# One block of a transformer on one NeuronCore: the second token tile of four pairs turned on VectorE instead of TensorE, with features dealt 5p+b

## The chip, the cores and the metric

The kernel runs on one core of one Trainium2 chip. The metric is the device time of one execution in microseconds (us); smaller is better. Three runs of the kernel before gave 762.3, 762.86 and 761.41 us, with a median of 762.3 us. The engines are named as the profile names them: PE is TensorE's matmul, PEld its weight load, DVE is VectorE, ACT is ScalarE, POOL is GpSimd, and SP is the engine whose queue issues most transfers.

## The reference

The kernel computes one block with two halves, conditioned by a vector c, for S = 2048 tokens of D = 640 features. All arrays are fp32.

```python
mod = silu(c) @ w_mod                      # six vectors of 640: sa, ca, ga, sb, cb, gb
h = layernorm(x) * (1 + ca) + sa
q, k, v = h @ wqkv                         # 32 heads of 20
phi_q = concat(softmax(q @ w_phi), softmax(-q @ w_phi))     # by head; phi_k alike
o = phi_q @ (phi_k.T @ v) / (phi_q @ sum(phi_k))
x = x + ga * (o @ wo)
h = layernorm(x) * (1 + cb) + sb
x = x + gb * (relu(h @ w1 + b1)**2 @ w2 + b2)
```

## The kernel before

**Tiles.** Tokens stand in 16 tiles of 128, and two tiles make a pair j (0 to 7). Matmuls contract over the partitions, so LayerNorm's result, which has tokens on the partitions, has to be turned first: 640 features are five chunks d = 0 to 4 of 128. Every fp32 factor is split into a high part and a rest (`hi`, written by ACT, and `lo`, the difference, written by DVE), and a product is three matmuls: hi by hi, hi by lo, lo by hi. That is `three`, and `proj` strings 15 of them (5 chunks by 3) for the first 384 output columns and 15 for the other 256.

**Phase 1** is the loop over tiles t = 2 to 13 (j, i = t // 2, t % 2), behind a start written by hand for pairs 0 and 1. For each tile PE does k, v and q, each with `proj`. In the tile with i = 0 it also adds the products of keys and values of the two tiles before (`do_kv`, output `kvp`). In between PE turns the next pair: chunks 0 and 1 behind q of the first tile (`t1(j + 1, 0, 1)`), chunks 2 and 3 between v and q of the second, and chunk 4 inside q of the second, 12 matmuls before its end. The next thing on PE is k of the next pair's first tile, which reads all five chunks in order.

`t1` is `t_in` (one transpose on PE for each tile and chunk, into the PSUM tile `ta`) and `t_out`: ACT writes `hf` = scaled and shifted `ta` (128x256, both tiles at once), ACT copies `hf` into `hT` (the high part), DVE subtracts (`lo`, the rest).

**LayerNorm** of a pair is `ln_parts`: sums on ACT, a factor on POOL, squares on ACT, three small operations on POOL, and a scaling of both tiles on ACT. It ran in the pair's predecessor, in the tile with i = 0.

**DVE** in phase 1 has, for each tile: maxima and minima by head of k and q (`mxk`, `mxq`), differences (`ek`, `eq`), sums of the exponentials (`sk`, `rs_q`), the reciprocal, the normalization of `ek` by `sk`, and `lo` of `hT`. It also sums w_mod by rows (`wm`) and prepares wo (`rwo`).

**What sets the order.** PE's order in the loop is the program's (`manual_schedule` for PE alone). DVE, ACT, POOL and SP are ordered by the scheduler, which simulates a timeline; each engine then runs its list strictly in that order.

**Where features stand.** Before, chunk d of phase 1 is features 128d to 128d+127. The second half of the kernel already uses the other order, chunk b holding features 5p+b (`by_turn`), and from its pair 1 on has its turns done by DVE in 32x32 blocks (`turn`, `ln_dealt`, `load_dealt`).

Of the kernel before, what the change touches and what calls it, by code (L numbers as in the profile page):

```python
# [21 lines left out]
NT = S // P  # L22
NC = D // P
# [9 lines left out]
EPS = 1e-5  # L33
# [19 lines left out]
def kernel(  # L53
# [54 lines left out]
    def tok2(tag, name, at=0, pool=None):  # L108

        bufs = 1  # L110
        if tag == "w":
            tag = f"w{next(w_at)}"
        elif pool is None:
            bufs = BUFS.get(tag, 1)
        t = (pool or mem).tile([P, 2 * D + (W2_AT if tag == 'late' else 128 if tag in W_LONG else 0)], F32, tag=tag, name=name, bufs=bufs)
        return t[:, at : at + 2 * D].rearrange("p (s d) -> p s d", s=2)

    def row(tag, name):
        return (pc if tag in ("s3", "s4") else mem).tile([P, D], F32, tag=tag, name=name, bufs=BUFS[tag])
# [7 lines left out]
    def ht(name, j, at=(32, 0)):  # L127

        t = mem.tile([P, NC * 512 + (32, 96)[j % 2]], F32R, tag=f"h{j % 2}", name=name, bufs=1)
        at = at[j % 2]  # L130
        return t[:, at : at + NC * 512].rearrange("p (d s n) -> p d s n", d=NC, s=2)

    def small(shape, tag, name, bufs=2):
        return (pc if tag in ("mx", "sk", "dn", "dd") else tiny).tile(shape, F32, tag=tag, name=name, bufs=bufs)
# [4 lines left out]
    def tp(name):  # L139
        return psA.tile([P, 512], F32, tag="tp", name=name)  # L140
# [80 lines left out]
    def load_x(j):  # L221
        XB[j] = tok2(f"x{j % 2}", f"xb{j}")
        nc.sync.dma_start(XB[j], x[256 * j : 256 * j + 256].rearrange("(i p) d -> p i d", p=P))

    def load_wm(d):
        WM[d] = flat(tok2(("k", "k", "q0", "q1", "w")[d], f"wm_{d}"))
# [106 lines left out]
    def ln_parts(xt, nm, spare=None):  # L333
        sm = small([P, 2], "sm", f"sm{nm}")
        sq = small([P, 2], "sq", f"sq{nm}")
        nb = small([P, 2], "nb", f"nb{nm}")
        for i in range(2):
            same = spare[i] if spare else xt[:, i] if nm[0] == "a" else row("s3", f"same{nm}_{i}")
            nc.scalar.activation(same, xt[:, i], AF.Identity, accum_out=sm[:, i : i + 1])
        nc.gpsimd.tensor_scalar(sm, sm, -1.0 / D, None, op0=ALU.mult)  # L340
        yield
        for i in range(2):
            junk = spare[i] if spare else row("s3", f"junk{nm}_{i}")
            nc.scalar.activation(junk, xt[:, i], AF.Square, bias=sm[:, i : i + 1], accum_out=sq[:, i : i + 1])
        nc.gpsimd.tensor_scalar(sq, sq, 1.0 / D, EPS, op0=ALU.mult, op1=ALU.add)
        nc.gpsimd.tensor_tensor(sq, sq, mhalf, op=ALU.pow)
        nc.gpsimd.tensor_tensor(nb, sm, sq, op=ALU.mult)
        yield
        for i in range(2):
            nc.scalar.activation(xt[:, i], xt[:, i], AF.Identity, bias=nb[:, i : i + 1], scale=sq[:, i : i + 1])  # L350
        yield

    def layer_norm(xt, nm, spare=None):
        for _ in ln_parts(xt, nm, spare):
            pass

    def by_turn(ap):
        return ap.rearrange("p (f b) -> p b f", b=NC)

    def t_in(xn, d, p, mixed=False):  # L360
        for i in range(2):
            src = by_turn(xn[:, i])[:, d] if mixed else xn[:, i, d * P : (d + 1) * P]
            nc.tensor.transpose(p[:, i * P : (i + 1) * P], src, ident)  # L363

    def t_unit(xn, cols, hT, d, nm, p=None):
        if p is None:
            p = tp(f"t{nm}_{d}")
        t_in(xn, d, p, True)
        t_out(cols, hT, d, nm, p)

    def t_out(cols, hT, d, nm, p, hf=None):
        if hf is None:
            hf = row("s3", f"hf{nm}_{d}")[:, :256]
        nc.scalar.activation(hf, p[:, :256], AF.Identity, bias=cols[:, d : d + 1], scale=cols[:, 5 + d : 6 + d])
        nc.scalar.activation(hT[:, d, 0], hf, AF.Copy)
        lo(hT[:, d, 1], hf, hT[:, d, 0])

# [5 lines left out]
    def newest(engine):  # L383
        return next(i for i in reversed(nc.cur_bb.bb.instructions) if i.engine == engine)

    DONE = []

    def t1(j, *ds, more=None):
        if 0 in ds:
            HT[j] = ht(f"hT{j}", j)  # L390
        p = tp(f"ta{j}_{ds[0]}")
        for k, d in enumerate(ds):
            t_in(XB[j], d, p[:, 256 * k : 256 * k + 256])
        if more:
            mod_turn(more[0], p[:, 256:], 4)
        for k, d in enumerate(ds):
            t_out(cols_a, HT[j], d, f"a{j}", p[:, 256 * k : 256 * k + 256])
        DONE[:] = newest(ET_.Activation), newest(ET_.DVE)
        if more:
            mod_sum(*more)  # L400

    def proj(nm, t, between=None):
        p = pj(f"p{nm}{t}")
        j, i = divmod(t, 2)
        s = slice(i * P, (i + 1) * P)
        for h, (a, b) in enumerate(CUT):
            terms = []
            for d in range(NC):
                w = W[nm, d]
# [308 lines left out]
    for t in range(2, NT - 2):  # L718
        j, i = divmod(t, 2)
        if i == 0 and j < NT // 2 - 2:  # L720
            load_x(j + 2)
        PK[t] = row("s2", f"k{t}")
        to_sb(proj("k", t), PK[t])
        if t == NT - 4:
            t1(j + 1, 0, 1)
        norm = j + 1 if i == 0 and t < NT - 4 else j + 2 if t == NT - 5 else None
        if norm:
            if not i:
                parts = ln_parts(XB[norm], f"a{norm}")
            with tc.issue_after(newest(ET_.Activation)):  # L730
                next(parts)
        p = proj("v", t, (1, 0, lambda: t1(j + 1, 4)) if t == NT - 3 else None)
        if i == 0:
            do_kv(t - 2)
            do_kv(t - 1)
            if t in AFTER_KV:
                AFTER_KV[t]()
        v_out(t, p)
        if norm and not i:
            next(parts)  # L740
        EK[t] = tok2("k", f"ek{t}")
        spread(PK[t], EK[t], f"k{t}")
        exps(EK[t])
        if norm and not i:
            next(parts)
        if i and t < NT - 4:
            t1(j + 1, 2, 3)
        with tc.issue_after(newest(ET_.DVE)):
            k_norm(EK[t], t)
        if t < NT - POSTPONED:  # L750
            do_q(t, (1, 3, lambda: t1(j + 1, 4, more=LAST_COL.get(t))) if i else None)
            if norm and i:
                with tc.issue_after(newest(ET_.Activation)), tc.issue_after(DONE[0]):
# [12 lines left out]
        SIDE[t]()  # L766
# [305 lines left out]
    def t2(j, *ds):  # L1072
        if 0 in ds:
            H2[j] = ht(f"h2_{j}", j, (0, 96))
        if j == 0:
            t_unit(XM[j], cols_b, H2[j], ds[0], f"b{j}", bank(f"tb{j}_{ds[0]}"))
            return
        if j in DEALT:
            for d in ds:
                hf = XM[j].rearrange("p s d -> p (s d)")[:, 256 * d : 256 * d + 256]  # L1080
                t_out(cols_b, H2[j], d, f"b{j}", hf, hf)
            return
        p = tp(f"tb{j}_{ds[0]}")
        for k, d in enumerate(ds):
            t_in(XM[j], d, p[:, 256 * k : 256 * k + 256], True)
        for k, d in enumerate(ds):
            t_out(cols_b, H2[j], d, f"b{j}", p[:, 256 * k : 256 * k + 256], XX[j][d % 2][:, :256])

# [663 lines left out]
```

## Time and profile before

| | us |
|---|---|
| median of three runs | 762.3 |
| lowest, highest | 761.41, 762.86 |
| the profiled execution, device time | 760.53 |
| its span, first to last instruction | 758.8 |
| phase 1's loop, in the span | about 60 to 226 |
| PE busy there | 166.00 of 166.00 |
| DVE busy there | 148.09 of 166.00 |
| ACT busy there | 113.92 of 166.00 |

All durations used below come from the one profiled execution, and its time is 1.8 us under the median of the runs. A row of the timeline gives start, length, engine, line, operation, output and input, shape and count; in square brackets stands how long the engine was idle before and who released it. Consecutive instructions of one engine overlap a little, so steps are taken from start to start.

### The profile page before, as it was taken

To read this page: it belongs to the slowest core of one execution; us is meant where nothing else is said; L and a number is where in the kernel's file an instruction comes from. 1 tells how busy PE (TensorE), PEld (TensorE's weight loads), DVE (VectorE), ACT (ScalarE), POOL (GpSimd) and SP (SyncE) were. 2 spreads that over 40 slices of the span, in tenths; PEclk is the share of its full clock that TensorE was granted. 3 is DMA by queue.
4 is the path that set the end of the run, shared out by engine and by line. 5 is a ranking of instruction groups with operands and counts; after the bars stand their busy time and mean duration, and the time that the engine had idled before them with its cause. 6 is when DMAs were issued, how large, how long until landed. Compare 5 with 4: busy or idle time off the path is not lost.

```text
span 758.8 us, 15386 instructions
## 1 busy us (share of the span) xinstructions
PE 751.5 (99%) x5898; PEld 732.2 (96%) x5898; DVE 605.3 (80%) x1121; ACT 456.7 (60%) x1054; POOL 168.7 (22%) x349
## 2 busy tenths in 40 slices
PE   9999999999999999999999999999999999999997
PEld 9999999999999988998999999999999999999997
DVE  6598997988999899998655868777777776777766
ACT  5767666677853365555777656466474756647431
POOL 3001101011100247543413020132221313213110
PEclk9999999999999999999999999999999999999999
DMA  9812431342332354644886555997677777767461
GB/s 328 329 57 83 139 105 54 105 137 103 137 105 94 94 167 149 164 105 105 208 206 213 141 191 212 283 273 214 186 206 209 205 196 201 207 177 216 125 182 36
DMA packets 57778, 126.04 MB, mean 166 GB/s; under 512 B 7324, under 2 KB 15265, under 8 KB 57705
## 3 DMA queue, kind: packets, MB, share of 16 engines
q1 hardware_dynamic: 37554, 78.75, 31.5%
q0 software_dynamic: 17568, 41.00, 21.9%
q10 hardware_dynamic: 2583, 5.30, 1.8%
q8 instruction: 46, 0.75, 0.4%
q14 instruction: 27, 0.22, 0.1%
HBM read 100.29 MB, written 29.89 MB: 172 GB/s over the span
## 4 chain that ended last, share of the span: by engine, by line
PE 87%; DVE 9%; ACT 3%; issue 1%; POOL 0%; DVEq 0%; POOLq 0%
PE up L79 22%; PE acc L79 16%; PE pq L79 9%; PE pk L79 9%; PE pv L79 9%; PE pwo L79 6%; PE acc3x L79 4%; PE kvp L455 3%; PE te L925 1%; DVE dn L883 1%; DVE scr L881 1%; DVE ezb L905 1%; PE ta L363 1%; DVE ot L89 1%; PE foldq L281 1%
## 5 line engine op out<-in xcount | busy, mean ns | idle before, releaser
L79 PE MATMUL up<-h,w 128*128 128x256 f32 x1640 | 204.6, 277 | 1.2 <-ACT ft L1268 0.9
L79 PEld LDWEIGHTS up<-h,w 128*128 128x128 f32 x1640 | 196.3, 188 | 2.1 <-ACT ft L1268 1.2
L1268 ACT ACTIVATE ft<-up,b_t 128x256 f32<-128x256 f32 x104 | 48.8, 470 | 97.4 <-PE up L79 97.2
L79 PE MATMUL acc<-w,ra 128*128 128x384 f32 x452 | 97.9, 336 | 0.6 <-DVE ra L89 0.6
L79 PE MATMUL pwo<-wo,ot 128*128 128x256 f32 (+3 forms) x512 | 80.6, 312 | 0.1
L1269 DVE TENSOR_TENSOR ft<-ft 128x256 f32<-128x256 f32 x104 | 43.9, 422 | 44.2 <-ACT ft L1268 42.8
L79 PEld LDWEIGHTS pwo<-wo,ot 128*128 128x128 f32 (+1 forms) x512 | 74.4, 188 | 3.2 <-issue 2.7
L79 PE MATMUL pq<-wq,hT 128*128 128x384 f32 (+1 forms) x480 | 75.1, 312 | 0.0
L79 PEld LDWEIGHTS acc<-w,ra 128*128 128x128 f32 x452 | 72.8, 188 | 1.9 <-DVE ra L89 1.7
L79 PE MATMUL pk<-wk,hT 128*128 128x384 f32 (+1 forms) x480 | 72.7, 309 | 0.0
L79 PE MATMUL pv<-wv,hT 128*128 128x384 f32 (+1 forms) x480 | 71.6, 307 | 0.0
L79 PEld LDWEIGHTS pq<-wq,hT 128*128 128x128 f32 x480 | 71.0, 188 | 0.6 <-issue 0.2
L79 PEld LDWEIGHTS pk<-wk,hT 128*128 128x128 f32 x480 | 70.5, 188 | 0.4 <-issue 0.2
L79 PEld LDWEIGHTS pv<-wv,hT 128*128 128x128 f32 x480 | 70.0, 188 | 0.0
L89 DVE TENSOR_TENSOR ra<-ft,ra 128x384 fp32r<-128x384 f32 (+2 forms) x86 | 36.8, 449 | 32.5 <-ACT ra L1292 19.9
L1378 POOL DMA_DIRECT2D ring_a<-td_a x34 | 18.5, 544 | 116.7 <-PE acc L79 105.6
L1292 ACT ACTIVATE ra<-ft 128x384 fp32r<-128x384 f32 x48 | 25.2, 526 | 28.4 <-DVE ft L1269 22.3
L79 PE MATMUL acc3x<-w,ra 128*128 128x256 f32 x231 | 39.8, 279 | 0.0
L79 PEld LDWEIGHTS acc3x<-w,ra 128*128 128x128 f32 x231 | 37.3, 188 | 0.2 <-DVE ra L89 0.2
L1283 DVE TENSOR_TENSOR ft<-ft 128x128 f32<-128x128 f32 x136 | 33.4, 287 | 1.2
L446 DVE TENSOR_REDUCE sk<-ek 128x64 f32<-128x1280 f32 x16 | 23.7, 1484 | 12.4 <-ACT ek L441 10.8
L889 POOL TENSOR_TENSOR dn<-dn,rs_q 128x32 f32<-128x32 f32 x32 | 20.1, 629 | 60.1 <-DVE dn L883 59.8
(274 smaller groups left out, 1454.1 us busy)
## 6 DMA issues: line engine op xcount, KB each, us to landing
ring_c<-td_c POOLq DMA_DIRECT2D x34, 384.0 KB, 3.9
ring_a<-td_a POOLq DMA_DIRECT2D x34, 384.0 KB, 3.4
ring_b<-td_b POOLq DMA_DIRECT2D x34, 256.0 KB, 3.4
esp<-eq SPq DMA_DIRECT2D x12, 640.0 KB, 3.1
el<-esp SPq DMA_DIRECT2D x12, 640.0 KB, 4.3
rw<-in_w SPq DMA_DIRECT2D x23, 320.0 KB, 3.5
wm<-in_w_mod SPq DMA_DIRECT2D x20, 320.0 KB, 3.4
xb<-in_x SPq DMA_DIRECT2D x8, 640.0 KB, 4.1
```

The source lines that it names most:

```text
L79: nc.tensor.matmul(o, a, b, start=first and i == 0, stop=last and i == len(terms) - 1, skip_group_check=skip,)
L89: (eng or nc.vector).tensor_tensor(out_lo, full, hi.bitcast(F32), op=ALU.subtract)
L281: nc.tensor.matmul(p[g // 3][:, (g % 3) * 120 : (g % 3) * 120 + n], r, bd_t[:120, g * 120 : g * 120 + n], start=True, stop=True,)
L363: nc.tensor.transpose(p[:, i * P : (i + 1) * P], src, ident)
L446: nc.vector.tensor_reduce(s, heads(flat(e)), axis=AX.X, op=ALU.add)
L455: nc.tensor.matmul(kvp[g // 4][64 * c : 64 * c + 64, a : a + 2 * n].rearrange("p (s n) -> p s n", s=2), v[:, u], e[:, :, o : o + n], start ...
L889: nc.gpsimd.tensor_tensor(dn[:, s], dn[:, s], rs[:, 1 - s], op=ALU.mult)
L1268: nc.scalar.activation(r, p, AF.Relu, bias=b1_t[:, f : f + 1])
L1269: nc.vector.tensor_tensor(r, r, r, op=ALU.mult)
L1283: nc.vector.tensor_tensor(t[:, o], t[:, a], t[:, b], op=op)
L1292: nc.scalar.activation(a[:, 0, :3], t[:, :3], AF.Copy)
L1378: nc.gpsimd.dma_start(RING[j, n, r], TD[n][r].bitcast(F32R))
```

## The change

Pairs 3 to 6 (`EARLY_DEALT`) no longer have their second tile turned by PE. Its x is loaded a second time, dealt over the partitions by four transfers: 32 tokens to a group of partitions, four runs of 160 features. `dealt_parts` replaces `ln_parts` for these pairs. It starts one tile earlier, in the second tile of pair j-2. POOL copies each token's two factors to where the dealt rows need them (16 copies of 32x4), ACT scales the dealt tile in four pieces of 160 columns, and one DVE transpose of 32x32 blocks writes the turned tile over the second half of `xb`. So that a block transpose yields whole chunks, all of phase 1 now has chunk b hold features 5p+b, and the weights and modulation rows are put in that order on the host. PE's remaining transposes read every fifth column. `t_out` has two inputs for these pairs, `ta` for the first tile and `xb` for the second, so its one 128x256 ACT operation becomes two of 128x128.

```diff
+EARLY_DEALT = range(3, NT // 2 - 1)
     def load_x(j):
         XB[j] = tok2(f"x{j % 2}", f"xb{j}")
         nc.sync.dma_start(XB[j], x[256 * j : 256 * j + 256].rearrange("(i p) d -> p i d", p=P))
+        if j in EARLY_DEALT:
+            XD[j] = row("s4", f"xd{j}")
+            for q in range(4):
+                nc.sync.dma_start(
+                    XD[j][32 * q : 32 * q + 32].rearrange("t (a c) -> t a c", a=4),
+                    x[256 * j + P : 256 * j + 2 * P, 160 * q : 160 * q + 160].rearrange("(a t) c -> t a c", a=4),
+                )
+    def dealt_parts(j):
+        xt, junk = XB[j], row("s3", f"junka{j}")
+        sm = small([P, 2], "sm", f"sma{j}")
+        rn = tiny.tile([P, 2, 2], F32, tag="rn", name=f"rna{j}", bufs=1)
+        ra = tiny.tile([P, 4, 2, 2], F32, tag="rna", name=f"rnaa{j}", bufs=1)
+        sq, nb = rn[:, :, 0], rn[:, :, 1]
+        for i in range(2):
+            nc.scalar.activation(junk, xt[:, i], AF.Identity, accum_out=sm[:, i : i + 1])
+        nc.gpsimd.tensor_scalar(sm, sm, -1.0 / D, None, op0=ALU.mult)
+        yield
+        for i in range(2):
+            nc.scalar.activation(junk, xt[:, i], AF.Square, bias=sm[:, i : i + 1], accum_out=rn[:, i, 0:1])
+        nc.gpsimd.tensor_scalar(sq, sq, 1.0 / D, EPS, op0=ALU.mult, op1=ALU.add)
+        nc.gpsimd.tensor_tensor(sq, sq, mhalf, op=ALU.pow)
+        nc.gpsimd.tensor_tensor(nb, sm, sq, op=ALU.mult)
+        for a in range(4):
+            for q in range(4):
+                nc.gpsimd.tensor_copy(ra[32 * q : 32 * q + 32, a], rn[32 * a : 32 * a + 32])
+        yield
+        for a in range(4):
+            d = XD[j][:, 160 * a : 160 * a + 160]
+            nc.scalar.activation(d, d, AF.Identity, bias=ra[:, a, 1, 1:2], scale=ra[:, a, 1, 0:1])
+        yield
+        nc.scalar.activation(xt[:, 0], xt[:, 0], AF.Identity, bias=rn[:, 0, 1:2], scale=rn[:, 0, 0:1])
+        yield
+        with tc.issue_after(newest(ET_.DVE)):
+            nc.vector.transpose(xt[:, 1].rearrange("p (b a t) -> p a b t", b=NC, t=32), XD[j].rearrange("p (a t b) -> p a b t", a=4, t=32))
+        yield
-    def t_in(xn, d, p, mixed=False):
-        for i in range(2):
-            src = by_turn(xn[:, i])[:, d] if mixed else xn[:, i, d * P : (d + 1) * P]
-            nc.tensor.transpose(p[:, i * P : (i + 1) * P], src, ident)
+    def t_in(xn, d, p):
+        for i in range(xn.shape[1]):
+            nc.tensor.transpose(p[:, i * P : (i + 1) * P], by_turn(xn[:, i])[:, d], ident)
...
-        nc.scalar.activation(hf, p[:, :256], AF.Identity, bias=cols[:, d : d + 1], scale=cols[:, 5 + d : 6 + d])
+        for o, p in ((hf, p[:, :256]),) if second is None else ((hf[:, :P], p[:, :P]), (hf[:, P:], second)):
+            nc.scalar.activation(o, p, AF.Identity, bias=cols[:, d : d + 1], scale=cols[:, 5 + d : 6 + d])
...
+        deal = i and j + 2 in EARLY_DEALT
+        if deal:
+            DEAL[j + 2] = dealt_parts(j + 2)
+            with tc.issue_after(newest(ET_.Activation)):
+                next(DEAL[j + 2])
```

**What moves on ACT and DVE.** The scheduler orders both anew. The three places below lie where PE goes from q of a pair's second tile to k of the next pair. First, ACT at t = 7 (pair 3's second tile), from the turn of chunks 2 and 3 to that of chunk 4, before (`hfa_2` to `hfa_4` are `hf` of the chunks, `ek` the exponentials of k, `mt` a modulation column):

```order
L374 ACTIVATE hfa_2_1777<-ta_2_1772,cols_a 128x256
L374 ACTIVATE hfa_3_1781<-ta_2_1772,cols_a 128x256
L441 ACTIVATE ek_1764<-ek_1764 128x640
L375 ACTIVATE hT_1673<-hfa_2_1777 128x256
L375 ACTIVATE hT_1673<-hfa_3_1781 128x256
L442 ACTIVATE ek_1764<-ek_1764 128x640
L431 ACTIVATE q_1831<-pq_0_1789 128x384
L308 ACTIVATE mt_1597<-ta_4_1809 128x128
L374 ACTIVATE hfa_4_1814<-ta_4_1809,cols_a 128x256
L375 ACTIVATE hT_1673<-hfa_4_1814 128x256
```

and now, from the second piece of chunk 3 on (ahead of it stand the two pieces `hfa_2<-ta_2` and `hfa_3<-ta_2`, with one `ek` between them):

```order
L411 ACTIVATE hfa_3_1861<-xb_1188,cols_a 128x128
L372 ACTIVATE junka_1781,rna_1783<-xb_1556,sma_1782 128x640
L412 ACTIVATE hT_1726<-hfa_2_1856 128x256
L412 ACTIVATE hT_1726<-hfa_3_1861 128x256
L469 ACTIVATE q_1912<-pq_0_1870 128x384
L479 ACTIVATE ek_1845<-ek_1845 128x640
L316 ACTIVATE mt_1657<-ta_4_1890 128x128
L411 ACTIVATE hfa_4_1894<-ta_4_1890,cols_a 128x128
L411 ACTIVATE hfa_4_1894<-xb_1188,cols_a 128x128
L469 ACTIVATE q_1912<-pq_1_1871 128x256
L384 ACTIVATE xb_1556<-xb_1556,rna_1783 128x640
L412 ACTIVATE hT_1726<-hfa_4_1894 128x256
```

The high part of chunk 4 (the last row) now has a square, the eviction of q's last columns and the scaling of the pair after next's first tile ahead of it, and the second `ek` stands behind q's first columns.

DVE at the same place, before:

```order
L438 TENSOR_TENSOR ek_1764<-k_1693,mxk_1765 128x640
L89 TENSOR_TENSOR hT_1673<-hfa_2_1777,hT_1673 128x256
L89 TENSOR_TENSOR hT_1673<-hfa_3_1781,hT_1673 128x256
L446 TENSOR_REDUCE sk_1785<-ek_1764 128x64
L89 TENSOR_TENSOR hT_1673<-hfa_4_1814,hT_1673 128x256
L312 TENSOR_REDUCE gate_a<-mt_1597 128x5
L447 RECIPROCAL sk_1785<-sk_1785 128x64
```

and now:

```order
L476 TENSOR_TENSOR ek_1845<-k_1746,mxk_1846 128x640
L90 TENSOR_TENSOR hT_1726<-hfa_2_1856,hT_1726 128x256
L90 TENSOR_TENSOR hT_1726<-hfa_3_1861,hT_1726 128x256
L484 TENSOR_REDUCE sk_1866<-ek_1845 128x64
L485 RECIPROCAL sk_1866<-sk_1866 128x64
L486 TENSOR_TENSOR ek_1845<-ek_1845,sk_1866 128x1280
L90 TENSOR_TENSOR hT_1726<-hfa_4_1894,hT_1726 128x256
```

The rest of chunk 4 moved behind the reciprocal and the normalization of `ek`. At t = 3, 5, 9 and 11 it still stands directly behind the sum `sk`.

Third, ACT at t = 5 (pair 2's second tile), before:

```order
L375 ACTIVATE hT_1322<-hfa_2_1426 128x256
L375 ACTIVATE hT_1322<-hfa_3_1430 128x256
L441 ACTIVATE ek_1413<-ek_1413 128x640
L442 ACTIVATE ek_1413<-ek_1413 128x640
L431 ACTIVATE q_1477<-pq_0_1438 128x384
L374 ACTIVATE hfa_4_1461<-ta_4_1458,cols_a 128x256
L375 ACTIVATE hT_1322<-hfa_4_1461 128x256
```

and now:

```order
L372 ACTIVATE junka_1406,rna_1408<-xb_1188,sma_1407 128x640
L479 ACTIVATE ek_1470<-ek_1470 128x640
L412 ACTIVATE hT_1351<-hfa_2_1481 128x256
L412 ACTIVATE hT_1351<-hfa_3_1486 128x256
L469 ACTIVATE q_1534<-pq_0_1495 128x384
L411 ACTIVATE hfa_4_1517<-xb_808,cols_a 128x128
L411 ACTIVATE hfa_4_1517<-ta_4_1515,cols_a 128x128
L480 ACTIVATE ek_1470<-ek_1470 128x640
L384 ACTIVATE xb_1188<-xb_1188,rna_1408 128x640
L469 ACTIVATE q_1534<-pq_1_1496 128x256
L412 ACTIVATE hT_1351<-hfa_4_1517 128x256
```

The same pieces as at t = 7 came ahead of chunk 4's high part here, without `mt`.

More of the change, by code (lines that the diff above doesn't have):

```diff
@@ L209 @@
     bd_t = row("s4", "bd_t")
-    raw, WM, RV, XB = {}, {}, {}, {}
+    raw, WM, RV, XB, XD = {}, {}, {}, {}, {}
     def load_raw(nm, w5, w1, ds=range(NC)):
@@ L367, in t_unit, with t_out @@
             p = tp(f"t{nm}_{d}")
-        t_in(xn, d, p, True)
+        t_in(xn, d, p)
         t_out(cols, hT, d, nm, p)
-    def t_out(cols, hT, d, nm, p, hf=None):
+    def t_out(cols, hT, d, nm, p, hf=None, second=None):
         if hf is None:
             hf = row("s3", f"hf{nm}_{d}")[:, :256]
-        nc.scalar.activation(hf, p[:, :256], AF.Identity, bias=cols[:, d : d + 1], scale=cols[:, 5 + d : 6 + d])
+        for o, p in ((hf, p[:, :256]),) if second is None else ((hf[:, :P], p[:, :P]), (hf[:, P:], second)):
+            nc.scalar.activation(o, p, AF.Identity, bias=cols[:, d : d + 1], scale=cols[:, 5 + d : 6 + d])
         nc.scalar.activation(hT[:, d, 0], hf, AF.Copy)
@@ L384, in newest @@
         return next(i for i in reversed(nc.cur_bb.bb.instructions) if i.engine == engine)
-    DONE = []
+    DONE, DEAL = [], {}
     def t1(j, *ds, more=None):
@@ L390, in t1 @@
             HT[j] = ht(f"hT{j}", j)
+        turned = j in EARLY_DEALT
         p = tp(f"ta{j}_{ds[0]}")
         for k, d in enumerate(ds):
-            t_in(XB[j], d, p[:, 256 * k : 256 * k + 256])
+            t_in(XB[j][:, :1] if turned else XB[j], d, p[:, 256 * k : 256 * k + 256])
         if more:
@@ L396, in t1 @@
         for k, d in enumerate(ds):
-            t_out(cols_a, HT[j], d, f"a{j}", p[:, 256 * k : 256 * k + 256])
+            t_out(cols_a, HT[j], d, f"a{j}", p[:, 256 * k : 256 * k + 256], None, XB[j][:, 1, P * d : P * d + P] if turned else None)
         DONE[:] = newest(ET_.Activation), newest(ET_.DVE)
@@ L728 @@
             if not i:
-                parts = ln_parts(XB[norm], f"a{norm}")
+                parts = DEAL.get(norm) or ln_parts(XB[norm], f"a{norm}")
             with tc.issue_after(newest(ET_.Activation)):
                 next(parts)
+        deal = i and j + 2 in EARLY_DEALT
[3 more added lines that the diff above has]
+                next(DEAL[j + 2])
         p = proj("v", t, (1, 0, lambda: t1(j + 1, 4)) if t == NT - 3 else None)
@@ L740 @@
             next(parts)
+        if deal:
+            next(DEAL[j + 2])
         EK[t] = tok2("k", f"ek{t}")
@@ L1084, in t2 @@
         for k, d in enumerate(ds):
-            t_in(XM[j], d, p[:, 256 * k : 256 * k + 256], True)
+            t_in(XM[j], d, p[:, 256 * k : 256 * k + 256])
         for k, d in enumerate(ds):
@@ L1711, with by_row @@
     b1[F:] = B_b1[F - FS[-1] :]
+    def by_row(w):
+        return w.reshape(P, NC, -1).transpose(1, 0, 2).reshape(D, -1)
     def by_chunk(w):
@@ L1716, in by_chunk @@
         t[:120] = w.T[:600].reshape(5, 120, D).transpose(1, 0, 2)
-        return t.reshape(P, 5, NC, P).transpose(2, 0, 1, 3).reshape(NC * P, D), w.T[600:]
+        return t.reshape(P, 5, P, NC).transpose(3, 0, 1, 2).reshape(NC * P, D), by_row(w)[:, 600:].T
     wq5, wq1 = by_chunk(A_wqkv[:, :D])
@@ L1722 @@
     w1 = np.stack([np.tile(w, (1, P // w.shape[1])).reshape(P, NC, P) for w in w1])
-    w_ss = w_mod[:, : 2 * D].reshape(NC, P, 2, NC, P).transpose(3, 1, 0, 2, 4).reshape(NC * P, 2 * D)
+    w_ss = w_mod[:, : 2 * D].reshape(NC, P, 2, P, NC).transpose(4, 1, 0, 2, 3).reshape(NC * P, 2 * D)
     given = {
@@ L1729 @@
         "wq1": wq1,
-        "wv": A_wqkv[:, 2 * D :][:, VCOLS],
+        "wv": by_row(A_wqkv[:, 2 * D :][:, VCOLS]),
         "bd": bd.reshape(120, 120),
```

## The prediction

> **What bounds the kernel now.** I read first the page's busy times, then PE's waits, then the window of phase 1's loop.
>
> ```profile
> PE 751.5 (99%) x5898; PEld 732.2 (96%) x5898; DVE 605.3 (80%) x1121; ACT 456.7 (60%) x1054; POOL 168.7 (22%) x349
> ...
> PE warm L630 <- POOL bdc L156: 1.1, 1, 1.1
> PE up L79 <- ACT ft L1268: 0.9, 1, 0.9
> ...
> 60.00:226.00 166.00, 166.00 (x1319) 164.66 (x1318) 148.09 (x191) 113.92 (x261) 17.26 (x28) 1.00 0.33 109
> ```
>
> PE's longest waits in the whole execution are 1.1 and 0.9 us, at the start and in phase 3, and inside phase 1's loop it is busy without a gap (the window is PE, PEld, DVE, ACT, POOL in this order, then the granted clock, 1.00). So PE's own work sets the time there, and the change can gain only what it takes off PE. DVE has 17.9 us idle in these 166, ACT 52. Neither is a bound by its sum, but both run strictly in order, so what matters is when a single result that PE wants comes out of its list. That is where I looked longest.
>
> **PE's work.** The start of one group to the start of the next gives what PE really spends:
>
> ```profile
> 97.19 0.60 PE L363 MATMUL ta<-ident,xb 128*128 128x128 f32 x4
> 97.54 4.62 PE L79 MATMUL pk<-wk,hT 128*128 128x384 f32 x30
> 102.00 4.47 PE L79 MATMUL pv<-wv,hT 128*128 128x384 f32 x30
> ...
> 111.36 4.46 PE L79 MATMUL pk<-wk,hT 128*128 128x384 f32 x30
> 115.66 4.46 PE L79 MATMUL pv<-wv,hT 128*128 128x384 f32 x30
> ```
>
> Four transposes take 97.54 - 97.19 = 0.35 us, at least 0.09 each. The 30 matmuls of k behind them take 4.46 us, against 4.30 (111.36 to 115.66) where no transpose stands before; with that 0.16 it is 0.51 us, at most 0.13 each. I take the middle, 0.11. Twenty transposes go (four pairs, five chunks): 20 x 0.11 = 2.2 us off PE, with bounds of 1.8 and 2.6.
>
> The 60 transposes that stay read every fifth column. The later transposes of `xm` already do so:
>
> ```profile
> 384.79 0.62 PE L363 MATMUL tb<-ident,xm 128*128 128x128 f32 x4
> 385.17 1.20 PE L79 MATMUL pwo<-wo,ot 128*128 128x256 f32 x8
> ```
>
> Four of them take 0.38 us against 0.35: 0.008 each, 60 x 0.008 = 0.5 us more. PE's net is -1.7 us.
>
> **What ACT, DVE, POOL and SP get.** Prices from the nearest rows:
>
> ```profile
> L1104 DVE STREAM_TRANSPOSE xm<-xx 128x640 f32<-128x640 f32 x14 | 19.1, 1364 | 0.0
> ...
> L1562 ACT ACTIVATE xx<-xx,rna 128x160 f32<-128x160 f32 x56 | 24.6, 509 | 0.7 <-DVE ft L1269 0.6
> L374 ACT ACTIVATE hfa<-ta,cols_a 128x256 f32<-128x256 f32 x30 | 15.6, 562 | 1.0 <-PE ta L363 0.7
> L350 ACT ACTIVATE xb<-xb,nba,sqa 128x640 f32<-128x640 f32 x12 | 10.4, 914 | 3.3 <-POOL nba L347 3.3
> L344 ACT ACTIVATE junka<-xb,sma 128x640 f32<-128x640 f32 x12 | 9.8, 819 | 0.0
> ...
> 405.78 5.97 POOL L1553 COPY rna<-rn 32x4 f32<-32x4 f32 x16
> ```
>
> DVE gets four block transposes, 4 x 1.36 = 5.5 us. Each stands behind the differences `ek` of a pair's first tile, where DVE waits for ACT's exponentials anyway (2.85 us in the row of 126.95 below), so I cost them nothing; without that cover they would be 1.4 us a pair on DVE. VectorE: DVE Perf Modes in the Trainium skill, section "Rules for kernel authors", advises TensorE for a 128x128 transpose where PSUM will do, and VectorE for 32x32 blocks. By that advice, counted as engine time, a tile costs 5 x 0.11 = 0.55 us on PE and 1.36 on DVE, and the change would lose 0.8 us four times, 3.2 us. The window above speaks against that count: the time that has room is DVE's, not PE's. POOL's 16 copies take up to 6.0 us a pair, hidden by the half tile (about 7 us) between the squares and the scaling that needs them; without cover, rival C. SP gets 16 issues, 12 of them at the start, ahead of pair 2's x:
>
> ```profile
> 25.28 0.38 SPq L223 DMA_DIRECT2D xb<-in_x  x1
> ...
> 56.51 0.73 ACT L339 ACTIVATE xb<-xb 128x640 f32<-128x640 f32 x1
> ```
>
> 12 x 0.4 = 5 us later still leaves 26 us before the first reader: nothing. The other transfers behind them on that queue are no sooner needed. Uncovered, it would be 5 us once.
>
> ACT has the weak point. A piece of 128 columns with scale and bias is not in the trace. The line through 160 columns (509 ns) and 640 (914) gives 0.844 ns a column and 0.48 us for 128; rows in sequence overlap by 0.1, so a step is 0.38 us. Bounds: 0.15, the step of the plain 128x128 copy `mt` below, and 0.46, that of the 128x256 form. A chunk then takes two steps (0.76) for one of 0.46.
>
> **Where this lands.** Chunk 4 is turned 12 matmuls before k of the next pair begins, and k needs its high part as its 13th matmul. From 4.30 us for 15 x 640 columns, 12 of 384 take 2.06 us, and the rest is needed two matmuls (0.34) later. Rows of before at t = 7:
>
> ```profile
> 134.24 0.74 ACT L441 ACTIVATE eq<-eq 128x640 f32<-128x640 f32 x1 [1.43 <-DVE eq L438]
> ...
> 136.81 0.37 ACT L425 ACTIVATE vt<-pv 128x240 f32<-128x240 f32 x1 [0.66 <-PE pv L79]
> ...
> 137.25 1.02 ACT L374 ACTIVATE hfa<-ta,cols_a 128x256 f32<-128x256 f32 x2
> 138.21 0.74 ACT L441 ACTIVATE ek<-ek 128x640 f32<-128x640 f32 x1
> 138.85 0.71 ACT L375 ACTIVATE hT<-hfa 128x256 fp32r<-128x256 f32 x2
> 140.34 0.74 ACT L442 ACTIVATE ek<-ek 128x640 f32<-128x640 f32 x1 [0.78 <-DVE ek L438]
> 140.99 0.47 ACT L431 ACTIVATE q<-pq 128x384 f32<-128x384 f32 x1
> 141.36 0.27 ACT L308 ACTIVATE mt<-ta 128x128 f32<-128x128 f32 x1
> ...
> 142.11 0.42 ACT L375 ACTIVATE hT<-hfa 128x256 fp32r<-128x256 f32 x1
> ```
>
> ```profile
> 126.95 1.49 DVE L446 TENSOR_REDUCE sk<-ek 128x64 f32<-128x1280 f32 x1 [2.85 <-ACT ek L441]
> 128.47 0.55 DVE L447 RECIPROCAL sk<-sk 128x64 f32<-128x64 f32 x1
> 129.06 1.49 DVE L448 TENSOR_TENSOR ek<-ek,sk 128x1280 f32<-128x1280 f32 x1
> ...
> 142.56 0.42 DVE L89 TENSOR_TENSOR hT<-hfa,hT 128x256 fp32r<-128x256 f32 x1
> ```
>
> ```profile
> 141.73 4.46 PE L79 MATMUL pk<-wk,hT 128*128 128x384 f32 x30
> ```
>
> Before, the high part was ready at 142.53 and the rest at 142.98, needed at 143.8 and 144.1: 1.1 us of room.
>
> Now ACT gets two sums and a square of LayerNorm and a piece ahead of the last evictions of v, about 2.6 us where it waited 1.43 + 0.66; with PE 0.3 earlier the stretch from `hfa_2` on begins at 137.4. Up to chunk 4's high part it has five pieces (1.90), two `ek` (138.21 to 138.85: 0.64 each), a square (0.82), two `hT` (0.62), q's first columns (0.37), `mt` (0.15), q's last columns (0.3, a step like those of `hT`) and a scaling (0.81): 6.25 us. It begins at 143.65 and is ready at 144.05. PE, 0.55 us earlier by the pair's transposes, wants it at 141.2 + 2.06 = 143.25: a **stall of 0.8**. The second `ek` ends at 137.4 + 3.59 + 0.73 = 141.7. Then DVE does `sk` (1.52), the reciprocal (0.59), the normalization (1.4) and only then chunk 4's rest (0.42): ready at 145.65, wanted 0.34 behind 144.05: **1.3 more**. Together 2.1. A stall one pair earlier moves PE later but not all of DVE and ACT, so I take 1.8.
>
> At t = 5 the same pieces without `mt` (6.10) begin at about 107.05, a tenth behind this row:
>
> ```profile
> 106.95 1.02 ACT L374 ACTIVATE hfa<-ta,cols_a 128x256 f32<-128x256 f32 x2
> ```
>
> High part ready at 113.55, wanted at 111.36 - 0.55 + 2.06 = 112.85: 0.7. DVE has only `sk` ahead there: `ek` ends at 112.15, the rest is ready at 114.1, wanted at 113.9: 0.2. Together 0.9. At t = 9 and 11 the squares stand further ahead and chunk 4's second piece is done early; the same count ends within 0.3 of the need, and at t = 3 the chunks are still whole: 0.3 for the three.
>
> Stalls 0.9 + 1.8 + 0.3 = 3.0; **sum -1.7 + 3.0 = +1.3 us**. The profiled execution would go from 760.53 to 761.8; its time is 1.8 under the runs' median, so on the median's scale it is 762.3 + 1.3 = 763.6. With pieces of 0.15 the stalls shrink to about 1.0, all at t = 7, and the sum is -0.7; with 0.46 they are 1.3 and 2.3, and with room gone at t = 9 and 11 (1.4) they are 5.0 and the sum is +3.3. Own range: 761.6 to 765.6.
>
> **The rivals.**
>
> B, not slower: ACT reaches chunk 4 in time. For it: ACT waits 52 us of 166, so its list may close up more than I allow, and most of a scheduler's order can be absorbed. Against it: at t = 7 even an `ek` at its old 140.34 puts chunk 4's rest at 141.1 + 3.93 = 145.0, over a microsecond late, unless DVE reaches the difference sooner. The deciding point is whether the second `ek` at t = 7 ends before 139.7. PE's saving then stands, at -1.7 to -0.7: 760.6 to 761.6.
>
> C, the factors come late: 16 copies take 6.0 us, against 16 x 0.18 at their median, so something holds POOL.
>
> ```profile
> L1553 POOL COPY rna<-rn x32: 176/182/834, 405.8 to 454.6; 32x4 f32<-32x4 f32 x32
> ...
> 120.64 0.65 POOL L345 TENSOR_SCALAR sqa<-sqa 128x2 f32<-128x2 f32 x1 [2.66 <-ACT junka L344]
> ...
> 122.81 0.60 POOL L347 TENSOR_TENSOR nba<-sma,sqa 128x2 f32<-128x2 f32 x1
> ```
>
> From the end of the squares at t = 5 (about 109), POOL's three small operations (2.8 us in these rows) and 6.0 of copies end at 117.8; the scaling's turn on ACT is at 116.6. It would then block both exponentials of q and DVE's `rs_q` behind it: 1.2 us less of room, some 0.6 at each of four pairs, 2.4 on top: 766.0. SBUF — State Buffer in the Trainium skill, section "SBUF: two separate sides", says that a DVE operation with two SBUF inputs and a GpSimd operation that reads SBUF lock each other out for a whole instruction; the 834 ns beside 182 agree with it.
>
> D, the transposes weren't PE's loss: matmul ends are modelled, and a hidden wait behind `ta` might stay. Then nothing is saved and 0.5 + 3.0 added: 765.8. Against it: the 4.30 and 4.46 us repeat.
>
> **How the numbers follow.** Forecast 0.50, B 0.27, C 0.15, D 0.08. What a measurement here tells from no change is about 0.2%, 1.5 us. Of the forecast's half 0.20 lie within that and 0.30 above; B gives 0.15 faster and 0.12 the same; C and D are slower. Faster 0.15, same 0.32, slower 0.53. The range runs from B's saving to C, 760.5 to 766.2.
>
> **What would show it.** PE's waits should name `pk` waiting for ACT `hT` and DVE `hT` at t = 7 to 8, about 2 us, and half as much at 5 to 6; phase 1's matmul groups of `ta` should number 40 transposes. If `pk` waits nowhere, I am wrong by B; if ACT waits for POOL `rnaa`, C; if DVE idles under 1 us a pair with `kvp` late, the block transposes weren't covered.

## The result, and the profile after

The changed kernel takes 764.97 us (median of seven runs, 762.27 to 765.97) where the kernel before takes 762.3 (seven runs, 761.19 to 762.91): a ratio of 1.0033, 95% interval 1.002 to 1.0046. A second measurement (`after_again` below) gave 764.36 us and a ratio of 1.0038 (1.0023 to 1.0053). The profiled execution of the change took 762.27 us with a span of 760.6, which is 1.7 and 1.8 us more than the one before. It is the shortest of its seven runs, and the profiles differ by less than the medians.

PE's waits after, in total, count and longest, and the window of phase 1's loop:

```profile
PE pk L80 <- DVE hT L90: 1.1, 1, 1.1
...
PE pk L80 <- ACT hT L412: 0.2, 1, 0.2
...
60.00:226.00 166.00, 164.58 (x1294) 161.73 (x1293) 151.09 (x193) 120.27 (x292) 28.89 (x92) 1.00 0.34 109
```

Two waits inside the loop are new, both of `pk` for `hT`, and PE is no longer busy for the whole window. Its rows of `ta` number 40 transposes, as forecast. PE's timeline after has them at t = 6 and t = 8:

```profile
111.78 2.24 PE L80 MATMUL pk<-wk,hT 128*128 128x384 f32 x12
114.24 2.61 PE L80 MATMUL pk<-wk,hT 128*128 128x384 f32 x18 [0.22 <-ACT hT L412]
116.69 4.46 PE L80 MATMUL pv<-wv,hT 128*128 128x384 f32 x30
...
142.28 2.92 PE L80 MATMUL pk<-wk,hT 128*128 128x384 f32 x14
146.26 2.21 PE L80 MATMUL pk<-wk,hT 128*128 128x384 f32 x16 [1.06 <-DVE hT L90]
148.31 1.91 PE L80 MATMUL pv<-wv,hT 128*128 128x384 f32 x10
```

From the first `pk` to the first `pv`, k of t = 6 takes 4.91 us and k of t = 8 6.03, against 4.30 before. The wait comes after 12 matmuls the first time (the high part of chunk 4) and after 14 the second time (its rest). The waits in brackets are shorter than what k loses (0.61 and 1.73 us), since the profile models where a matmul ends; k's length is the better measure. ACT and DVE at t = 7, after:

```profile
141.49 0.75 ACT L480 ACTIVATE ek<-ek 128x640 f32<-128x640 f32 x1
142.12 0.29 ACT L316 ACTIVATE mt<-ta 128x128 f32<-128x128 f32 x1
142.28 0.48 ACT L411 ACTIVATE hfa<-ta,cols_a 128x128 f32<-128x128 f32 x1
142.62 0.52 ACT L411 ACTIVATE hfa<-xb,cols_a 128x128 f32<-128x128 f32 x1
143.00 0.40 ACT L469 ACTIVATE q<-pq 128x256 f32<-128x256 f32 x1
143.27 0.95 ACT L384 ACTIVATE xb<-xb,rna 128x640 f32<-128x640 f32 x1
144.08 0.44 ACT L412 ACTIVATE hT<-hfa 128x256 fp32r<-128x256 f32 x1
```

```profile
142.27 1.49 DVE L484 TENSOR_REDUCE sk<-ek 128x64 f32<-128x1280 f32 x1 [0.55 <-ACT ek L480]
143.79 0.55 DVE L485 RECIPROCAL sk<-sk 128x64 f32<-128x64 f32 x1
144.38 1.49 DVE L486 TENSOR_TENSOR ek<-ek,sk 128x1280 f32<-128x1280 f32 x1
145.79 0.42 DVE L90 TENSOR_TENSOR hT<-hfa,hT 128x256 fp32r<-128x256 f32 x1
```

The high part was ready at 144.52, and PE wanted it at 142.28 + 2.06 = 144.34, so ACT was 0.2 us late. The rest was ready at 146.21, since DVE did the reciprocal and the normalization first, and it was wanted 0.34 us behind the high part, at 144.86. By these rows most of the 1.73 us is DVE's order, and `dve_order` below puts it to the test.

### The profile page after: what moved, and what is told of

It is laid out like the page before. It is cut to its first block, busy times and chain, and to the rows that moved or that the text cites. A ratio compares the mean times of both kernels' runs of the same rounds, so it can differ in the third digit from the quotient of the medians.

```text
span 760.6 us, 15464 instructions
## 1 busy us (share of the span) xinstructions
PE 751.7 (99%) x5878; PEld 730.6 (96%) x5878; DVE 609.3 (80%) x1125; ACT 464.0 (61%) x1086; POOL 180.7 (24%) x413
## 4 chain that ended last, share of the span: by engine, by line
PE 83%; DVE 10%; ACT 6%; issue 1%; POOL 0%; DVEq 0%; POOLq 0%
PE up L80 22%; PE acc L80 16%; PE pk L80 8%; PE pv L80 8%; PE pq L80 8%; PE pwo L80 6%; PE acc3x L80 4%; PE kvp L493 3%; PE te L970 1%; DVE dn L928 1%; DVE scr L926 1%; DVE ezb L950 1%; DVE ot L90 1%; PE foldq L289 1%; PE foldk L289 1%
## 5 line engine op out<-in xcount | busy, mean ns | idle before, releaser
L1423 POOL DMA_DIRECT2D ring_b<-td_b x34 | 18.3, 538 | 48.7 <-PE acc L80 44.6
```

Of the source, the lines that this page charges most:

```text
L1423: nc.gpsimd.dma_start(RING[j, n, r], TD[n][r].bitcast(F32R))
```

## The experiments

Each kernel was timed in turn with the kernel before, on the same chip. To compare profiles without the noise of the first 14 us (the last folded weights begin between 13.2 and 14.1 us, presumably as `wq` arrives), I measure the loop on PE from the first `kvp` of t = 2 to the `kvp` of t = 14. In the three profiles of kernels whose phase 1 is that of before, this is 171.78 us each time.

**Only the new feature order** (`strided_only`).

```diff
-EARLY_DEALT = range(3, NT // 2 - 1)
+EARLY_DEALT = range(0)
```

> Only the order 5p+b and the transposes that read every fifth column are kept; no pair is turned on VectorE, no second load of x, no copies on POOL. ACT's and DVE's orders are those of before. Theory (the transposes' read costs 0.008 us each, 80 of them): span +0.6 us over 758.8, of it about 0.2 by the first kvp of t = 2; k's 30 matmuls take 4.3 us from their first to v's first at every pair where no transpose stands between. Rival S (the 0.6 us that the changed kernel had lost ahead of the loop comes from the twelve more loads at the start): span +0.3 and nothing lost ahead of the loop. Rival L (the new layout itself costs, in the folding of weights or the columns of the modulation): +1.5 us or more, most of it ahead of the loop.

Measured: 762.49 us (761.65 to 765.31, 12 runs), ratio 1.0014 (1.0001 to 1.0028); span 761.1. First and last `kvp` on PE's timeline, before and with only the order:

```profile
60.42 2.54 PE L455 MATMUL kvp<-ek,vt 128*64 128x120 f32 x44
232.20 2.54 PE L455 MATMUL kvp<-ek,vt 128*64 128x120 f32 x44
```

```profile
18.79 1.43 PE L399 MATMUL kvp<-ident,xb 128*128 128x128 f32 x10
20.06 0.27 PE L642 MATMUL kvp<-ident,msb 128*128 128x128 f32 x1
...
61.31 2.54 PE L493 MATMUL kvp<-ek,vt 128*64 128x120 f32 x44
233.50 2.54 PE L493 MATMUL kvp<-ek,vt 128*64 128x120 f32 x44
```

The loop is 172.19 us long, 0.41 more for 60 transposes: 0.007 each. Ahead of the loop ten transposes take 20.06 - 18.79 = 1.27 us, against 1.15 before (18.22 to 19.37), so 0.012 each. Together about 0.65 us for 80. The rest of the +2.3 in the span is the later start of the last folded weights (0.6) and 1.0 us that PE loses behind 390 us, to which the later experiments come. Rival S is out: time is lost ahead of the loop without the additional loads. From the start of the last folded weights to the first `kvp` of t = 2, `strided_only` takes 47.42 us and `after_again`, which has the loads, 47.46, against 47.09 before. Rival L is out as well.

**DVE's order alone** (`dve_order`): in pairs 2 to 5, the reciprocal and the normalization of `ek` behind chunk 4's rest. `k_sums` and `k_scale` are the two halves of `k_norm`, and the other pairs keep it whole.

```diff
-        with tc.issue_after(newest(ET_.DVE)):
-            k_norm(EK[t], t)
+        late_norm = i and j + 1 in EARLY_DEALT
...
+            with tc.issue_after(newest(ET_.DVE)):
+                sk = k_sums(EK[t], t)
...
+            if late_norm:
+                with tc.issue_after(DONE[1]):
+                    k_scale(EK[t], sk)
```

> In pairs 2 to 5, second tile, the reciprocal and the normalization of ek are issued behind the rest (lo) of chunk 4; ACT keeps its order, with the scaling of the first tile ahead of chunk 4's high part. Theory (at t = 7 it is DVE's order that holds k): there the high part still comes at 144.5 where k wants it at 144.3, and the rest 0.4 behind it, so k's 30 matmuls of t = 8 go from 6.03 to about 4.6 us; those of t = 6 stay at 4.9, where ACT is late. Span 760.6 - 1.4 = 759.2, time about 1.4 us under that of the changed kernel. Rival A (ACT's late high part holds k, and DVE's difference only follows it): k at t = 8 stays over 5.4 us and the gain is under 0.6 us.

Measured: 767.95 us (767.85 to 768.67, 4 runs), ratio 1.0085 (1.0069 to 1.0101). The local forecast holds: PE's timeline shows

```profile
142.79 4.91 PE L80 MATMUL pk<-wk,hT 128*128 128x384 f32 x30
147.53 2.76 PE L80 MATMUL pv<-wv,hT 128*128 128x384 f32 x15
...
217.50 1.70 PE L499 MATMUL kvp<-ek,vt 128*64 128x120 f32 x22 [3.56 <-DVE ek L489]
219.13 1.12 PE L399 MATMUL ta<-ident,xb 128*128 128x128 f32 x4
219.91 5.43 PE L80 MATMUL pk<-wk,hT 128*128 128x384 f32 x30
```

so k of t = 8 takes 4.74 us (6.03 before this edit) while k of t = 6 stays at 4.83 and k of t = 10 goes from 4.66 to 4.88. ACT's high part of chunk 4 is as late here as in the changed kernel (ready 0.2 us behind PE's want): at t = 7 DVE's order cost 1.29 of the 1.73 us, and rival A is out. The span was missed by 6.9 us, above all because of t = 11. There the edit lets DVE's work on `ek` sink in its list: the sum begins at 207.62 us (204.38 in the changed kernel), the normalization at 215.87 (212.43), and `kvp` of t = 12 waits 3.56 us for it. Then PE's clock falls, as the windows show (PE, PEld, DVE, ACT, POOL, then the granted clock, DMA share, GB/s):

```profile
217.00:219.00 2.00, 1.50 (x22) 1.49 (x22) 2.00 (x4) 0.88 (x2) 0.00 (x0) 0.84 0.00 0
219.00:221.00 2.00, 2.00 (x10) 1.87 (x8) 1.93 (x2) 1.30 (x3) 0.00 (x0) 0.50 0.29 35
221.00:223.00 2.00, 2.00 (x11) 2.00 (x11) 1.93 (x3) 0.93 (x3) 0.00 (x0) 0.81 0.38 137
223.00:225.00 2.00, 2.00 (x18) 2.00 (x17) 0.90 (x3) 0.49 (x1) 0.00 (x0) 1.00 0.00 0
```

**ACT's order** (`act_order`): the scaling of the dealt pair's first tile behind v's evictions.

```diff
         if norm and not i:
-            next(parts)
+            if norm in EARLY_DEALT:
+                with tc.issue_after(newest(ET_.Activation)):
+                    next(parts)
+            else:
+                next(parts)
```

> The scaling of the dealt pair's first tile is put behind the evictions of v of the next tile on ACT, so it no longer stands ahead of chunk 4's high part; the scheduler then also leaves chunk 4's rest directly behind the sum sk on DVE at t = 7. Theory (chunk 4 late through the two orders, and nothing else): k's 30 matmuls take 4.3 to 4.5 us at t = 6, 8 and 10, for 4.91, 6.03 and 4.66 now; 2.74 us of stalls become under 0.6, span about 758.4, time 2.2 us under the changed kernel, level with the kernel before. Rival M (the wait moves on: with the scaling later, the pieces of chunks 0 and 1 or the products of keys and values wait): k is quick, but as much time is lost at other places, span over 759.8.

Measured: 761.31 us (759.85 to 764.75, 12 runs), ratio 0.9997 (0.9981 to 1.0014). PE's timeline:

```profile
61.02 2.54 PE L493 MATMUL kvp<-ek,vt 128*64 128x120 f32 x44
...
111.47 4.74 PE L80 MATMUL pk<-wk,hT 128*128 128x384 f32 x30
116.05 4.46 PE L80 MATMUL pv<-wv,hT 128*128 128x384 f32 x30
...
141.65 4.46 PE L80 MATMUL pk<-wk,hT 128*128 128x384 f32 x30
145.95 4.24 PE L80 MATMUL pv<-wv,hT 128*128 128x384 f32 x28
...
231.06 2.54 PE L493 MATMUL kvp<-ek,vt 128*64 128x120 f32 x44
```

k of t = 6 takes 4.58 us, of t = 8 and 10 4.30: the stalls are gone but for 0.28. DVE's rest of chunk 4 at t = 7 stands directly behind the sum again, as expected (143.11 behind 141.63 us). The loop is 170.04 us, 1.74 less than before and 2.81 less than in the changed kernel (172.85). The theory holds within phase 1, and rival M is out there. Its span of 758.4 did not come: this execution has 763.0. From the last `kvp` shown to the end it takes 531.9 us, against 526.6 before, and the loss stands behind 390 us.

**Both orders** (`both_orders`): as `act_order`, and the whole of `k_norm` behind chunk 4's rest.

> Both: the scaling behind the evictions of v on ACT, and on DVE the sum, reciprocal and normalization of ek behind chunk 4's rest. Theory: no stall at k, 4.3 us at t = 6, 8 and 10; PE's saving of 1.7 us then stands against what is lost ahead of the loop (0.6): span 757.9 to 758.2, 0.6 to 0.9 us under the kernel before. Rival N (k's sum and normalization a chunk later make kvp of the next tile wait for ek): PE waits for DVE ek ahead of kvp, up to 1 us at each of t = 6, 8, 10, and the span is 759.5 or more. Rival D of the prediction (turning fewer tiles on PE saves nothing): span 759.8 with no waits at k.

Measured: 769.88 us (769.0 to 771.74, 4 runs), ratio 1.0112 (1.0093 to 1.013). Rival N, several times larger than forecast: k of t = 6, 8 and 10 is quick (4.37, 4.30, 4.30), but `kvp` waits 5.4 us for `ek`, 4.9 of it at once at t = 12, and the clock falls behind it (0.50 from 217 to 223 us).

```profile
218.09 2.53 PE L499 MATMUL kvp<-ek,vt 128*64 128x120 f32 x22 [4.94 <-DVE ek L489]
```

**What is lost behind 390 us.** SP in the profile of before (first two rows), then SP, ACT and PE in that of `act_order`, then its windows:

```profile
388.37 0.27 SPq L1203 DMA_DIRECT2D gate<-gate_r  x1
390.35 0.32 SPq L1204 DMA_DIRECT2D gb_b<-gate  x1
...
387.27 0.27 SPq L1252 DMA_DIRECT2D gate<-gate_r  x1
393.71 0.32 SPq L1253 DMA_DIRECT2D gb_b<-gate  x1
...
398.68 0.74 ACT L1067 ACTIVATE w<-rw 128x640 fp32r<-128x640 f32 x1 [4.14 <-DMA rw<-in_w]
...
401.56 1.26 PE L80 MATMUL acc<-w,ra 128*128 128x384 f32 x3 [2.69 <-ACT ra L1341]
```

```profile
400.00:402.00 2.00, 0.43 (x2) 0.30 (x2) 1.16 (x3) 1.51 (x6) 0.00 (x0) 1.00 1.04 267
402.00:404.00 2.00, 2.00 (x9) 1.84 (x8) 1.13 (x3) 1.66 (x4) 0.22 (x1) 0.55 1.16 284
404.00:406.00 2.00, 2.00 (x12) 2.00 (x11) 1.08 (x2) 2.00 (x6) 0.00 (x0) 0.59 0.81 212
406.00:410.00 4.00, 4.00 (x34) 4.00 (x34) 2.58 (x6) 3.10 (x7) 2.72 (x9) 1.00 0.92 321
```

The vector `gate` is stored to DRAM and read back as `gb_b`, spread over the partitions. The read waits on SP until the store has landed, here 6.4 us, against 2.0 in the profile of before. Behind it on SP stand w1's and w2's loads `rw`, so ACT waits 4.1 us for one, PE 2.7 us for ACT, and then PE runs at 0.55 to 0.59 of its clock for 4 us. DMA: Bandwidth & Descriptors in the Trainium skill, section "Latency and other measured facts", puts the memory's access at 0.2 us on average and 2 us at high load, the main part of a transfer's fixed cost of some 2 us; 1.9 to 2.2 us in the shortest of the profiles below agree with it, 4.5 and 6.4 are beyond. To test whether this makes the longer runs, one issue was moved in three kernels, from right behind the store into the first pass of the second half. On SP it then stands behind twelve loads `rw` of w1 and w2 that came after it:

```diff
-            nc.sync.dma_start(gb_b, GD[1].rearrange("c p -> (c p)")[None, :].to_broadcast([P, D]))
...
+            if (j, n) == (0, 3):
+                nc.sync.dma_start(gb_b, GD[1].rearrange("c p -> (c p)")[None, :].to_broadcast([P, D]))
```

**The change again** (`after_again`), unaltered, beside them:

> The changed kernel once more, unaltered. Theory: its loop over t = 2 to 13 is 1.1 us longer than before's and the part ahead of it 0.3 to 0.7 longer (the transposes that read every fifth column, and the arrival of wq), so over many runs it is 1.4 to 1.8 us above the kernel before; what the seven first runs showed beyond that (2.7 by the medians) came from runs in which the load of gb_b, which waits on SP for the store of gate, came late and held up w1's and w2's loads behind it, as it did in the profile of act_order (about 3 to 4 us in such a run, in either kernel). Rival: all of the 2.7 us belongs to the change, and shows again.

Measured: 764.36 us (763.32 to 766.36, 6 runs). The loop is 172.59 us in this profile. All of the difference (2.67 us) is there again, so the theory's forecast for the time (1.4 to 1.8) missed: the longer runs are the rule in this kernel, not the exception.

**The load of gb_b moved in the kernel before** (`gate_before`):

> The kernel before, with one DMA issue moved on SP: the broadcast load of gb_b, which has to wait until the store of gate has landed, stands behind fourteen loads of w1 and w2 (in the first tile pair of the second half) and no longer ahead of them. Nothing else is touched. Theory (that wait is what makes some runs of every kernel 3 to 4 us longer): the lowest runs stay at about 760.5 us, and the runs above 762.5, eight of 23 so far, are gone; median 0.3 to 0.7 us lower. Rival J (the longer runs come from elsewhere): as many runs above 762.5 as before.

Measured: 760.91 us (760.41 to 761.45, 11 runs), ratio 0.9987 (0.9979 to 0.9996). Of 29 runs of the kernel before beside it, seven are over 762.5 us; of these 11, none. That speaks against rival J, and the next run decides it.

**Moved in the changed kernel** (`gate_after`):

> The same one move in the changed kernel. Theory: the long runs are gone and what is left against the kernel before with the same move is phase 1's 1.4 to 1.8 us; ratio to the kernel before about 1.001 to 1.002. Rival J: no change against after_again.

Measured: 762.19 us (761.33 to 763.0, 12 runs), ratio 1.0004 (0.9996 to 1.0013). It is 2.2 us under `after_again`, and the ranges do not overlap, so rival J is out. It is 1.28 over `gate_before`, with a loop of 172.73 us.

**Moved, with ACT's order** (`gate_act`):

> The same move together with the scaling put behind the evictions of v on ACT (as in act_order). Theory: PE is 1.1 to 1.4 us ahead of the kernel before when the loop ends, as in act_order, keeps it to the end now that no load waits behind gb_b, and no run is 3 us long: median about 759.3 to 759.8, 0.2% under the kernel before. Rival P (the loads of w1 and w2 are due at their own time, and a PE that is early waits for them): the lead is given back around 393 to 410 us of the span, and the median is level with gate_before.

Measured: 760.7 us (759.49 to 761.42, 11 runs), ratio 0.9984 (0.9974 to 0.9993); under the kernel before, but only 0.2 us under `gate_before`. Its profile has a loop of 170.61 us, 0.58 more than that of `gate_act2` below. All of this stands in t = 2 to 5, where k of t = 2 and 4 takes 4.39 us instead of 4.30 without a wait (4.39 and 4.34 in the profile after); why, no run shows. To decide, both were run again on another chip. **The kernel before, moved, again** (`gate_before2`):

> The kernel before with the load of gb_b moved, again, beside gate_act2 on the same chip. Expected level with its first measurement: 0.1% to 0.2% under the kernel before, no run above 762.5 us.

and **the changed one with both edits, again** (`gate_act2`):

> The changed kernel with the scaling behind the evictions of v and the load of gb_b moved, again. The loop over t = 2 to 13 was 1.2 to 1.7 us shorter than before's in the two profiles with this order, the part ahead of it 0.3 to 0.7 longer. Theory: the rest, 0.5 to 1.4 us, is a true gain, and the median is that much under gate_before2. Rival P: the lead is given back later, and the two medians are within 0.3 us of each other, as in the first measurement (760.70 and 760.91).

Measured: 761.36 us (760.6 to 762.38, 11 runs), ratio 0.9997 (0.9988 to 1.0006), and 759.87 (759.13 to 762.17, 11 runs), ratio 0.9979 (0.9969 to 0.9989). The first again has no run over 762.5 us (three of 21 of the kernel before beside it have), but its median is level with the kernel before, where 0.1% to 0.2% less was expected. PE's timeline and the loop's window of the second:

```profile
61.39 2.54 PE L493 MATMUL kvp<-ek,vt 128*64 128x120 f32 x44
...
231.42 2.54 PE L493 MATMUL kvp<-ek,vt 128*64 128x120 f32 x44
```

```profile
60.00:226.00 166.00, 166.00 (x1313) 164.39 (x1313) 154.63 (x197) 121.07 (x295) 28.10 (x93) 1.00 0.34 111
```

PE is busy throughout again, the loop is 170.03 us, and the lead lasts: the span is 758.2. Rival P is out: behind the loop this profile takes 526.8 us and that of `gate_act` 526.7, as `gate_before`'s does (526.75). This version was under the kernel before in both measurements, with the interval below 1 each time. Its lead on the kernel before with the same move was 0.2 us in one measurement and 1.5 in the other, so the size of the turn's own gain is known only roughly.

**Two more profiles of the changed kernel**, to catch a longer run in one (`after_look1`, `after_look2`):

> The changed kernel, one more profiled execution, to catch a long run. Theory: where the time is over 764 us, the load of gb_b is issued 4 us or more behind the store of gate (2 us in the two profiles so far), ACT waits for rw and PE's acc for ra by 2 to 3 us at about 400 us, and the granted clock falls under 0.7 for some 4 us behind it; phase 1's loop is the same as in the shorter runs. Rival: the 2 to 3 us are lost elsewhere, in phase 1 above all.

> A second look at the changed kernel, for the same question and with the same numbers: in a run over 764 us the load of gb_b 4 us or more behind the store of gate, acc waiting 2 to 3 us at about 400 us, the clock under 0.7 behind it; in a shorter run none of the three.

The first took 762.95 us and shows none of it. The second took 764.2, with a loop of 172.90 us like the first's; SP in it, and PE's wait:

```profile
389.97 0.27 SPq L1248 DMA_DIRECT2D gate<-gate_r  x1
394.46 0.32 SPq L1249 DMA_DIRECT2D gb_b<-gate  x1
```

```profile
PE acc L80 <- ACT ra L1337: 1.4, 1, 1.4
```

The place and the order of waits are right; the wait is 1.4 us for the 2 to 3 forecast, and the clock stays at 1.00 behind it, against the forecast. All nine profiles with `gb_b` at its old place (`rw` is the next load on SP):

| | store to load of `gb_b`, us | store to next `rw`, us | wait of `acc` for `ra`, us |
|---|---|---|---|
| after | 1.9 | 3.0 | none |
| before | 2.0 | 3.0 | none |
| strided_only | 2.2 | 3.0 | 0.2 |
| after_look1 | 2.4 | 3.0 | none |
| after_again | 2.6 | 3.1 | 0.2 |
| both_orders | 2.8 | 3.2 | 0.6 |
| dve_order | 3.0 | 3.5 | 0.2 |
| after_look2 | 4.5 | 4.9 | 1.4 |
| act_order | 6.4 | 6.9 | 2.7 |

In the five profiles with `gb_b` moved, `rw` follows the store after 3.0 us and `acc` never waits for `ra`. So the load of `gb_b` holds up the queue only when it comes later than `rw` would anyway, as in the last four rows. In `strided_only` and `after_again` `rw` was issued in time (within 0.1 us), and PE still waited 0.2 us, so SP's order is not all of it. The move also takes the 320 KB that `gb_b` reads away from this place, and no run separates the two.

## Why the prediction was right, and where it was short

The forecast was 763.6 us, in a range that holds the measured 764.97, with slower as the likeliest sign. Step by step:

- **Twenty transposes off PE, -2.2.** Right. The loop of `gate_act2` is 1.75 us shorter than before's (1.74 in `act_order`, 1.17 in `gate_act`); with the 0.26 that k of t = 6 still loses there (4.56 against 4.30) and the 0.27 that 40 strided transposes cost (0.007 each), that is 2.28 us for 20, 0.114 each (by `gate_act` about 1.6). Rival D is out.
- **Strided transposes, +0.5.** Right: 40 in the loop at 0.007 and 20 ahead of it at 0.012 are 0.52.
- **Chunk 4 late at t = 5 and 7, and the three others: 0.9, 1.8 and 0.3.** Measured by k's length: 0.61, 1.73 and 0.45 (0.36 of it at t = 10), 2.79 for 3.0. The split at t = 7 was off: I gave ACT 0.8 and DVE 1.3, but PE came to k 1.1 us later than I had reckoned, so ACT was only 0.2 late and DVE's reciprocal and normalization were most of the rest. About 0.3 us of the loop's +1.07 stays unassigned, most of it in t = 2 to 5 (50.74 us from the first `kvp` to k of t = 6, against 50.45 in `gate_act2`).
- **A piece of 128 columns, 0.48 us.** Right, as the profile after has it:

```profile
L411 ACT ACTIVATE hfa<-ta,cols_a x30: 452/472/576, 68.7 to 223.8; 128x128 f32<-128x128 f32 x20, 128x256 f32<-128x256 f32 x10
```

- **POOL's copies and the block transposes, nothing.** Right: 16 copies took 3.8 to 4.9 us a pair and ACT never waits for `rnaa`, so rival C did not come. ACT waits 1.0 us in all for a turned `xb` (0.5 at the longest), and PE does not feel it.
- **Rival B** failed at its deciding point: the second `ek` at t = 7 ended at 142.24, not before 139.7.
- **The sum, +1.3.** Without the longer runs it is what was measured: 762.19 - 760.91 = 1.28 us. So close an agreement is partly luck: `gate_before` had 760.91 us on one chip and 761.36 on another.

What was short is the step from the profile to the median: "its time is 1.8 under the runs' median, so on the median's scale it is 762.3 + 1.3". That assumed that the distance is the same in both kernels. In the changed kernel it was 2.7 (764.97 - 762.27), and what it has more goes with the place of `gb_b`'s load behind the store of `gate`: with the load moved, the excess is gone (from 764.36 to 762.19 us, where the kernel before goes from 761.69 to 760.91). Why the changed kernel meets that wait in more of its runs, some 190 us behind the last turn that it changes, no run has shown.

## What to carry to other kernels

Where an engine with room takes over work, look at the next result that the busiest engine wants and count what the new pieces put ahead of it on the strictly ordered engines: here 2.2 us of saved PE time became a loss through results that came 0.2 to 1.4 us late, and pinning one operation's place in ACT's order turned it into a loop that is 1.2 to 1.75 us shorter than before's. An order is pinned piece by piece: the same edit on DVE that mended t = 7 made PE wait 3.6 us for what it put off at t = 11. A round trip through DRAM on the queue that also feeds the weights was here a wait that differed from run to run by up to 4.5 us; before comparing changes of less than a percent, move its second half behind the loads.

## What the runs showed of the hardware

- **One wait of PE costs more than its length.** Behind waits of 1.06 and 1.4 us the granted clock stayed at 1.00. Behind 2.7 us it was 0.55 to 0.59 for 4 us, behind 4.94 us (`both_orders`) 0.50 for 6 us, and behind 3.56 us it was 0.84, 0.50 and 0.81 for 6 us: in `dve_order` k of t = 13 took from 219.91 to 225.17, 5.26 us, against 4.46 before. TensorE: Matmul & The Clock Gate in the Trainium skill, section "Part 1: The HAM clock gate (the "warmup" mystery)", says that the clock halves after an idle window of about 3.4 us; here 2.7 us were enough once.
- **A store of 2.5 KB let the load behind it wait 1.9 to 6.4 us** at the same place of the program, counted from issue to issue. The other such store, `gate_a` in phase 1, was followed by its load after 7.5 to 10.9 us in the fourteen profiles. In that of before the DMA engines were nearly idle meanwhile (a share of 0.00 to 0.16 from 144 to 154 us), and PE did not wait for it.
- **POOL's small copies** of 32x4, 180 ns at the median, took up to 1391 ns in the profile after. That one ran from 144.52 to 145.91 us, and DVE's normalization of `ek`, which reads two inputs from SBUF, from 144.38 to 145.87.
